# Decode attention on one core: TensorE's score matmuls rolled into an inner loop over pairs of groups, an empty first turn, and no loop aligned to a fetch block

## The chip, the cores and the metric

The kernel runs on one core of a Trainium2 chip. The metric is the device time of one execution in microseconds (us). Lower is better. The profile of the core lists five engines. The program has an instruction stream for each and orders them by semaphores: TensorE (PE; its weight loads are shown as PEld), VectorE (DVE), ScalarE (ACT), GpSimd (POOL) and SyncE (SP, which here issues the DMAs).

Every run in this study was in the fast state, with a granted TensorE clock of 1.000 wherever a profile gives it. The differences are small (under 0.3% in most runs), so most kernels were timed in five rounds beside runs of the kernel before on the same chip.

## The reference, cut to what matters

```python
B, Hq, Hkv, Sq, Sk, D = 1, 32, 8, 1, 65536, 128        # bf16
k = jnp.repeat(k, 4, axis=1); v = jnp.repeat(v, 4, axis=1)
scores = jnp.einsum("bhqd,bhkd->bhqk", q, k) * D ** -0.5
p = softmax(scores, axis=-1)
return jnp.einsum("bhqk,bhkd->bhqd", p, v)
```

There is one query per head, and 8 heads of K and V with 65536 rows each. K and V together are 268.4 MB and each byte is used once. The kernel cannot be faster than the stream of K and V from memory, 619.3 us at the 433.5 GB/s that the packets show (below).

## The kernel before

The work is cut into N = 16 chunks: 8 heads times 2 halves of 32768 rows. For each chunk, 8.39 MB of K and 8.39 MB of V are loaded. There are two K buffers and one V buffer. VectorE turns K by 16 transposes per chunk, one per "group" of 16 rows per partition, into two small buffers `ktb` used in turn. TensorE does 16 score matmuls per group into PSUM. ScalarE moves the scores out and takes the exponentials. TensorE then multiplies 256 weight tiles of V with them.

The DMA issues wait for the engines here:

```python
        def load_k(i):
            if i >= NK:
                sp.wait_ge(tr_s, (i - NK + 1) * G)      # K i-2 is transposed
            ...
        def load_v(i):
            if i < N - HALVED:
                if i >= 1:
                    sp.wait_ge(pv_s, 2 * i)             # values i-1 are done
                load(vbuf, vf, i, 0, T, v_in)
                return
            sp.wait_ge(pv_s, 2 * i - 1)                 # the last two V: in halves
            load(vbuf, vf, i, 0, TH, va_in)
            sp.wait_ge(pv_s, 2 * i)
            ...
```

TensorE before: one loop over chunks, aligned to a fetch block. The score matmuls of a chunk are written out, so their PSUM addresses are constants.

```python
        with nc.Fori(0, N + 1, 1, engines=..., head_slot={pe.engine: 0}) as it:
            ...                                          # registers of this turn
            hq = kept_ // C * QH
            qcols = [hq + be * A * R for be in range(NB * NE)]
            with pe.If_lt(turn, N):
                for g in range(G):                       # G = 16, unrolled
                    if g % GU == 0:
                        pe.wait_ge(mv_s, it * U + (g // GU + 1))
                    pe.wait_ge(tr_s, it * G + (g + 1))
                    scores(g, qcols)                     # 16 matmuls
            with pe.If_eq(skip, 0):                      # not in turn 0
                ...                                      # waits
                values(range(TH)) ...                    # 256 matmuls of chunk it-1
```

VectorE, for each group, waits until the score matmuls two groups back have read its buffer, and transposes:

```python
                    dv.wait_ge(qk_s, h * (C * G) + (b * G + g - NKT + 1))   # NKT = 2
                    transpose(b, g)
```

Of the kernel before, what the change touches and what calls it, by code (L numbers as in the profile page):

```python
# [5 lines left out]
DT = mybir.dt  # L6
AF = mybir.ActivationFunctionType
ALU = mybir.AluOpType
AX = mybir.AxisListType

P = 128
S4 = 32
T = 256
TG = 16
G = T // TG
U = 4
GU = G // U
NK = 2
NKT = 2
FIRST = (64, 64, 128)  # L20
KLAST = (128, 128)
VLAST = (72, 32, 16, 8)
NEND = 2
HALVED = 2


# [8 lines left out]
def bass_standalone__gqa_softmax__decode_kernel(nc, q, k, v, out):  # L35
    B, Hq, Sq, D = q.shape
    _, H, Sk, _ = k.shape
    R = Hq // H
    CK = P * T
    assert B == 1 and Sq == 1 and D == P and Hq == H * R == S4 and R == 4  # L40
    C = Sk // CK
    assert Sk % CK == 0 and C == 2
    N = H * C
    A = P // S4
    NB, NE = 2, 2
    W = T // U * R
    TH = T // 2
    QH = NB * NE * A * R
    scale = float(D) ** -0.5
    TE = sum(VLAST[-NEND:])  # L50
    assert sum(VLAST) == TH
# [5 lines left out]
    S = es.enter_context  # L57
# [6 lines left out]
    ktb = [sb(f"ktb{i}", [P, TG * D], DT.bfloat16) for i in range(NKT)]  # L64
# [23 lines left out]
    q4, qt = (scs[:, i * D // 2:(i + 1) * D // 2].bitcast(DT.bfloat16) for i in range(2))  # L88
    ident = ktb[0][:, 0:2 * P].bitcast(DT.float32)

    qkb = [S(nc.psum_tensor(f"qkb{i}", [P, 512], DT.float32)) for i in range(U)]
    acc = S(nc.psum_tensor("acc", [P, 512], DT.float32))

    def sem(name):
# [3 lines left out]
    v_in, va_in, vb_in = sem("v_in"), sem("va_in"), sem("vb_in")  # L98
    first_in = [sem(f"first_in{i}") for i in range(len(FIRST))]
    klast_in = [sem(f"klast_in{i}") for i in range(len(KLAST))]  # L100
    vlast_in = [sem(f"vlast_in{i}") for i in range(len(VLAST))]
# [12 lines left out]
    def pieces(sizes, at=0):  # L114
        for n, size in enumerate(sizes):
            yield n, at, at + size
            at += size
# [66 lines left out]

    @block.tensor
    def _(pe):
        def scores(g, qcols):


            kt = ktb[g % NKT][:, :].rearrange("p (b n e) -> p b e n", b=NB, e=NE)  # L190
            for n in range(TG // A):
                at = (g % GU * (TG // A) + n) * A * R
                for be in range(NB * NE):
                    ins = pe.matmul(  # L194
                        qkb[g // GU][:, at:at + A * R],
                        lhsT=kt[:, be // NE, be % NE, n * P:(n + 1) * P],
                        rhs=qblk[:, bass.ds(qcols[be], A * R)],
                        start=be == 0, stop=be == NB * NE - 1,
                    )
            ins.then_inc(qk_s, 1)  # L200

        def values(tiles):

            for t in tiles:
                ins = pe.matmul(  # L205
                    acc[:, 0:R], lhsT=vbuf[:, t * D:(t + 1) * D], rhs=pts[:, t * R:(t + 1) * R],
                    start=t == 0, stop=t == T - 1,
                )
                if t % TH == TH - 1:
                    ins.then_inc(pv_s, 1)  # L210


        turn, skip, skipl, late, last, kept, whole = (
            pe.alloc_register(name) for name in ("turn", "skip", "skipl", "late", "last", "kept", "whole"))
        pe.reg_mov(turn, 0)
        pe.wait_ge(qb_s, A * NB)
        with nc.Fori(
            0, N + 1, 1, engines=bass.OrderedEngineSet([pe.engine]), head_slot={pe.engine: 0},
        ) as it:
            pe.reg_alu(skip, it, 1, ALU.is_lt)  # L220
            pe.reg_alu(last, it, N, ALU.is_ge)
            pe.reg_alu(late, it, N - HALVED + 1, ALU.is_ge)
            pe.reg_add(skipl, skip, last)
            pe.reg_alu(kept, it, N - 1, ALU.min)
            pe.reg_alu(whole, it, N - HALVED, ALU.min)
            kept_ = pe.snap(kept, min_val=0, max_val=N - 1)
            whole_, late_, last_ = (pe.snap(r, min_val=0, max_val=N) for r in (whole, late, last))
            hq = kept_ // C * QH
            qcols = [hq + be * A * R for be in range(NB * NE)]
            with pe.If_lt(turn, N):  # L230
                for g in range(G):
                    if g % GU == 0:
                        pe.wait_ge(mv_s, it * U + (g // GU + 1))
                    pe.wait_ge(tr_s, it * G + (g + 1))
                    scores(g, qcols)
            with pe.If_eq(skip, 0):
                pe.wait_ge(co_s, it - 1)
                pe.wait_ge(ex_s, it * R)
                pe.wait_ge(v_in, whole_ * 16)
                pe.wait_ge(va_in, late_ * 16 + last_ * 16)  # L240
                values(range(TH))
                pe.wait_ge(vb_in, late_ * 16)
                for n, a, b in list(pieces(VLAST, TH))[:-NEND]:
                    pe.wait_ge(vlast_in[n], last_ * 16)
                    values(range(a, b))
            with pe.If_eq(skipl, 0):
                values(range(T - TE, T))
            pe.reg_add(turn, turn, 1)


        pe.wait_ge(tail_s, 2)
        pe.wait_ge(ow_s, H)
        pe.matmul(acc[:, 0:R], lhsT=ident, rhs=o2, start=False, stop=False)  # L253
        for n, a, b in list(pieces(VLAST, TH))[-NEND:]:
            pe.wait_ge(vlast_in[n], 16)
            values(range(a, b))

    @block.vector
    def _(dv):
# [47 lines left out]
            dv.alloc_register(name) for name in ("started", "before", "filled", "last"))  # L307


        with nc.Fori(0, H, 1, engines=bass.OrderedEngineSet([dv.engine]), head_slot={dv.engine: 0}) as h:  # L310
            dv.reg_alu(started, h, 1, ALU.is_ge)
            dv.reg_alu(last, h, H - 1, ALU.is_ge)
            dv.reg_alu(filled, h, 1, ALU.add)
            dv.reg_alu(filled, filled, H - 1, ALU.min)
            dv.reg_alu(before, h, -1, ALU.add)
            dv.reg_alu(before, before, 0, ALU.max)
            started_, last_ = dv.snap(started, min_val=0, max_val=1), dv.snap(last, min_val=0, max_val=1)
            filled_, before_ = dv.snap(filled, min_val=0, max_val=H - 1), dv.snap(before, min_val=0, max_val=H - 2)
            for b in range(C):
                dv.wait_ge(k_in[b], (filled_ if b else h) * 16)  # L320
                moved = h * (C * U) + (U + b * U + 1)
                for g in range(G):
                    for n, at, _ in pieces(KLAST if b else FIRST):
                        if at == g * TG:
                            dv.wait_ge((klast_in if b else first_in)[n], last_ * 16 if b else 16)
                    if b * G + g >= NKT:
                        dv.wait_ge(qk_s, h * (C * G) + (b * G + g - NKT + 1))  # L327
                    else:
                        dv.wait_ge(qk_s, h * (C * G) - started_ * (NKT - 1 - g))  # L329
                    transpose(b, g)  # L330
                    if g >= 2 * GU and g % GU == 0:
                        maximum(b, g // GU - 2, moved)
                for u in range(U - 2, U):
                    maximum(b, u, moved)
                dv.wait_ge(mx_s, h * (C * U) + (b + 1) * U)
                if b:
                    dv.wait_ge(hma_s, h * C + 1)
                dv.tensor_reduce(  # L338
                    hmax[:, b * R:(b + 1) * R], hp[b].rearrange("p (u g) -> p g u", g=R), AX.X, ALU.max,
                ).then_inc(hm_s, 1)  # L340
                if b:
                    dv.wait_ge(hma_s, h * C + 2)
                    dv.tensor_tensor(dif, mfirst, mtot, ALU.subtract).then_inc(df_s, 1)  # L343
                    dv.wait_ge(pv_s, h * (2 * C) + 2)
                    dv.tensor_copy(o1, acc[:, 0:R]).then_inc(co_s, 1)  # L345
                else:
                    with dv.If_eq(started, 1):
                        weigh(before_)
                        dv.wait_ge(pv_s, h * (2 * C))
                        dv.wait_ge(ow_s, h)  # L350
                        dv.tensor_tensor(o2, acc[:, 0:R], o2, ALU.add).then_inc(co_s, 1)  # L351
                        divisor(before_)
                        dv.wait_ge(co_s, h * C)
                        dv.tensor_tensor(oT[:, bass.ds(before_ * R, R)], o2, recip, ALU.mult).then_inc(fin_s, 1)  # L354
# [9 lines left out]
    def _(ac):  # L364
# [4 lines left out]
        ac.activation(warm[:, 8:9], warm[:, 9:10], AF.Exp, scale=1.0).then_inc(warm_s, 1)  # L369

        def move(b, u):
            fr = qkb[u][:, 0:W].rearrange("p (n a g) -> p a n g", a=A, g=R)
            to = scs[:, u * W:(u + 1) * W].rearrange("p (n x g) -> p x n g", x=A, g=R)
            for x in range(A):
                for a in range(A):
                    ins = ac.activation(to[a * S4:(a + 1) * S4, x, :, :], fr[x * S4:(x + 1) * S4, a, :, :], AF.Copy)  # L376
            ins.then_inc(mv_s, 1)


        with nc.Fori(0, H, 1, engines=bass.OrderedEngineSet([ac.engine]), head_slot={ac.engine: 0}) as h:  # L380
            for b in range(C):
                ac.wait_ge(ex_s, h * (C * R) + b * R)
                for u in range(U):
# [49 lines left out]
```

## Time and profile before

| | before |
|---|---|
| time, median | 629.28 us on the first three runs, 629.36 us with the three beside the kernel after |
| K and V moved | 268.45 MB; mean 428 GB/s over the span |
| busy: DVE / ACT / PE | 54% / 44% / 43% |
| mean rate in packets, 90 to 560 us | 433 GB/s |

From the page of the kernel before come the DMA rows in 40 slices and the costliest groups of instructions. In a group line the numbers after the bar are busy us and mean ns of one instruction; after the second bar comes the idle time before them and what ended most of it.

```profile
DMA  9999999999999999999999999999999999999997
GB/s 368 438 449 424 439 422 413 455 413 451 417 451 417 451 417 442 426 442 426 438 430 438 430 434 434 434 434 434 430 438 430 438 430 430 438 415 430 434 432 293
...
L276 DVE STREAM_TRANSPOSE ktb<-kbuf 128x1024 int32<-128x1024 int32 x256 | 295.7, 1212 | 155.8 <-DMA kbuf<-in_k_dram 142.3
...
L194 PE MATMUL qkb<-qblk,ktb 128*128 x4096 | 157.1, 176 | 341.4 <-DVE ktb L276 326.4
...
L205 PE MATMUL acc<-pts,vbuf 128*128 128x4 bf16 x4096 | 112.4, 166 | 14.1 <-DMA vbuf<-in_v_dram 13.4
```

The DMA engines are busy all the time and no other engine is. The large idle times are waits for data. The kernel is bound by the DMA stream: 268.45 MB at 433.5 GB/s take 619.3 us. The rest is the start, the end and any time at which the stream runs dry.

The chain of waits of the same kernel (start us, us, what) shows how one turn hangs together:

```profile
178.45 1.21 DVE ktb L276
179.71 0.59 PE qkb L194 x16
180.36 7.00 PE acc L205 x256
187.37 0.33 SPq L124
187.74 49.80 DMA kbuf<-in_k_dram
```

VectorE finishes the last transpose, TensorE the last scores and the values, then SP may issue the next V and K. The K so issued lands 49.8 us later, although 8.39 MB need only 19.4 us: the rest of the time it queues behind other transfers. The list of DMA issues (size or count, median us from issue to landing) says the same of V:

```profile
vbuf<-in_v_dram SPq DMA_DIRECT2D x14, 30.8
```

V needs 19.4 us of transfer, so it is issued while about 11 us of other load are still queued. As long as that queue does not run empty, time that TensorE loses costs nothing here.

There are two places where the queue is short. The first is early. Timeline of TensorE and SP (start us, us, engine, line, ..., count, [idle before, what ended it]):

```profile
52.48 1.32 PE L194 MATMUL qkb<-qblk,ktb 128*128 x32 [13.95 <-issue]
...
71.06 6.98 PE L205 MATMUL acc<-pts,vbuf 128*128 128x4 bf16 x256
...
78.08 0.33 SPq L124 DMA_DIRECT2D vbuf<-in_v_dram  x1
```

TensorE is idle for 14 us before its second chunk. One DMA queue, of the kind "instruction", carries nothing but five packets of 16 KB, about 1.0 us each; by their number and times they are TensorE's fetches. They start at 16.2, 31.6, 41.6, 48.6 and 55.9 us, the last three 7.0 and 7.3 us apart, with the DMA engines busy throughout (share 1.03 from 38 to 56 us); none comes later, though the loop runs 17 turns. The wait covers two of them. It makes the second V late (78.08 us), and the DMA engines then go partly idle.

The second place is the tail, where no K is left to load and the last V is loaded in halves, each waiting for values of the V before it. The timeline there:

```profile
596.36 0.59 PE L194 MATMUL qkb<-qblk,ktb 128*128 x16 [0.53 <-DVE ktb L276]
...
597.03 3.57 PE L205 MATMUL acc<-pts,vbuf 128*128 128x4 bf16 x128
600.63 10.22 SPq L124 DMA_DIRECT2D vbuf<-in_v_dram  x5
605.49 3.58 PE L205 MATMUL acc<-pts,vbuf 128*128 128x4 bf16 x128 [4.89 <-DMA vbuf<-in_v_dram]
```

The first half of the last V is issued at 600.63 us, when the first half of the values of chunk 14 is done. What was in flight then (the second half of V 14) lands at 605.49 us. The stream stays full, as the busy times of this stretch show (from, to, length; PE, PEld, DVE, ACT, POOL busy; clock; DMA share; GB/s):

```profile
600.00:610.00 10.00, 4.17 (x151) 4.00 (x148) 1.27 (x5) 1.89 (x8) 0.81 (x3) 1.00 1.01 433
```

### The profile page before, as it was taken

What the parts mean: (1) busy time and instruction counts of PE and PEld (TensorE: products, weight loads), DVE (VectorE), ACT (ScalarE), POOL (GpSimd) and SP (SyncE); (2) the same over time, 40 slices, a digit from 0 to 9 for tenths busy, and PEclk for the clock granted to TensorE, in tenths of its full rate; (3) what the DMA queues carried; (4) which work ended last, traced back from release to release, by engine and by line L of the source; (5) the groups of instructions that cost most, each with busy time, mean ns of one, the idle gap of its engine ahead of it and who ended that gap; (6) DMA issues with size and microseconds to landing.
All of it is one profiled execution on the core that took longest, in us unless ns stands there. A gap on an engine that the chain in (4) does not pass through costs nothing.

```text
span 628.1 us, 19282 instructions
## 1 busy us (share of the span) xinstructions
PE 269.9 (43%) x8194; PEld 243.9 (39%) x8194; DVE 341.2 (54%) x411; ACT 275.6 (44%) x1178; POOL 10.5 (2%) x32
## 2 busy tenths in 40 slices
PE   0323737144361534615346252452615526156445
PEld 0312636044361433614335152452514526146444
DVE  1865576290753908538094480935719357195910
ACT  0363645164351734517346172461725526264640
POOL 0000000000000000000000000000000000000000
DMA  9999999999999999999999999999999999999997
GB/s 368 438 449 424 439 422 413 455 413 451 417 451 417 451 417 442 426 442 426 438 430 438 430 434 434 434 434 434 430 438 430 438 430 430 438 415 430 434 432 293
DMA packets 6094, 268.60 MB, mean 428 GB/s; under 512 B 964, under 2 KB 964, under 8 KB 1220
## 3 DMA queue, kind: packets, MB, share of 16 engines
q1 hardware_dynamic: 5892, 268.45, 99.1%
q8 instruction: 5, 0.08, 0.1%
q10 hardware_dynamic: 192, 0.03, 0.0%
q14 instruction: 5, 0.04, 0.0%
HBM read 268.47 MB, written 0.01 MB: 427 GB/s over the span
## 4 chain that ended last, share of the span: by engine, by line
DMA 63%; DVE 16%; issue 10%; PE 10%; DVEq 0%; SPq 0%; ACTq 0%
DMA kbuf<-in_k_dram 55%; DVE ktb L276 14%; PE acc L205 9%; DMA vbuf<-in_v_dram 7%; DVE small L283 1%; DMA scs<-in_q_dram 1%; PE qkb L194 1%; SPq L124 0%; ACTq L366 0%; DVE qblk L271 0%; DVEq L329 0%; DVEq L327 0%; PE acc L253 0%; DVE scs L263 0%; DVE oTX L361 0%
## 5 line engine op out<-in xcount | busy, mean ns | idle before, releaser
L276 DVE STREAM_TRANSPOSE ktb<-kbuf 128x1024 int32<-128x1024 int32 x256 | 295.7, 1212 | 155.8 <-DMA kbuf<-in_k_dram 142.3
L376 ACT ACTIVATE scs<-qkb 32x64 f32<-32x64 f32 x1024 | 220.3, 215 | 280.2 <-PE qkb L194 269.0
L194 PE MATMUL qkb<-qblk,ktb 128*128 x4096 | 157.1, 176 | 341.4 <-DVE ktb L276 326.4
L194 PEld LDWEIGHTS qkb<-qblk,ktb 128*128 128x128 bf16 x4096 | 132.7, 105 | 365.7 <-issue 202.6
L205 PE MATMUL acc<-pts,vbuf 128*128 128x4 bf16 x4096 | 112.4, 166 | 14.1 <-DMA vbuf<-in_v_dram 13.4
L205 PEld LDWEIGHTS acc<-pts,vbuf 128*128 128x128 bf16 x4096 | 111.0, 104 | 15.7 <-DMA vbuf<-in_v_dram 11.6
L283 DVE TENSOR_REDUCE small<-scs 128x4 f32<-128x256 f32 x64 | 37.5, 586 | 61.4 <-ACT scs L376 61.4
L399 ACT ACTIVATE pts<-scs,small 128x256 bf16<-128x256 f32 x64 | 48.9, 853 | 30.7 <-PE acc L205 30.5
L171 POOL PARTITION_ALL_REDUCE small<-small x16 | 5.9, 370 | 589.9 <-DVE small L338 589.9
L399 ACT ACTIVATION_READ_ACCUMULATOR pts<-scs,small 128x1 f32 x64 | 13.6, 213 | 0.0
L387 ACT ACTIVATE small<-small 128x4 f32<-128x4 f32 x16 | 3.3, 206 | 22.5 <-POOL small L171 22.5
L345 DVE COPY small<-acc 128x4 f32<-128x4 f32 x8 | 1.3, 161 | 19.4 <-PE acc L205 19.4
L351 DVE TENSOR_TENSOR small<-acc,small 128x4 f32<-128x4 f32 x7 | 1.1, 163 | 13.8 <-PE acc L205 13.8
L359 DVE TENSOR_TENSOR oTX<-acc,small 128x4 bf16<-128x4 f32 x1 | 0.2, 163 | 12.3 <-PE acc L205 12.3
L263 DVE STREAM_TRANSPOSE scs<-scs 128x64 int32<-128x64 int32 x1 | 0.2, 246 | 9.8 <-DMA scs<-in_q_dram 9.8
L338 DVE TENSOR_REDUCE small<-small 128x4 f32<-128x16 f32 (+1 forms) x16 | 3.0, 185 | 1.3
L163 POOL PARTITION_ALL_REDUCE small<-small x8 | 3.4, 429 | 11.5 <-DVE small L296 11.5
L343 DVE TENSOR_TENSOR small<-small 128x4 f32<-128x4 f32 x8 | 1.3, 163 | 4.0 <-POOL small L171 4.0
L294 DVE TENSOR_TENSOR small<-small 128x4 f32<-128x4 f32 x8 | 1.3, 163 | 2.7 <-ACT pts L399 2.7
L369 ACT ACT_TABLE_LOAD x1 | 1.3, 1283 | 3.1 <-issue 3.1
L354 DVE TENSOR_TENSOR oTX<-small 128x4 f32 x7 | 1.1, 163 | 1.7 <-DVE small L300 1.7
L292 DVE TENSOR_TENSOR small<-small 128x4 f32<-128x4 f32 x8 | 1.4, 181 | 0.9
(18 smaller groups left out, 8.8 us busy)
## 6 DMA issues: line engine op xcount, KB each, us to landing
kbuf<-in_k_dram SPq DMA_DIRECT2D x3, 4096.0 KB, 40.2
vbuf<-in_v_dram SPq DMA_DIRECT2D x3, 4096.0 KB, 24.7
kbuf<-in_k_dram SPq DMA_DIRECT2D x2, 2048.0 KB, 10.3
vbuf<-in_v_dram SPq DMA_DIRECT2D x1, 2304.0 KB, 11.6
vbuf<-in_v_dram SPq DMA_DIRECT2D x1, 1024.0 KB, 13.7
vbuf<-in_v_dram SPq DMA_DIRECT2D x1, 512.0 KB, 14.5
vbuf<-in_v_dram SPq DMA_DIRECT2D x1, 256.0 KB, 14.6
kbuf<-in_k_dram SPq DMA_DIRECT2D x14, 49.8
```

Of the source, the lines that this page charges most:

```text
L163: g.partition_all_reduce(lsum, rhead, P, bass.bass_isa.ReduceOp.add).then_inc(ls_s, 1)
L171: g.partition_all_reduce(mtot if b else mfirst, hmax[:, b * R:(b + 1) * R], P, bass.bass_isa.ReduceOp.max,).then_inc(hma_s, 1)
L194: ins = pe.matmul(qkb[g // GU][:, at:at + A * R], lhsT=kt[:, be // NE, be % NE, n * P:(n + 1) * P], rhs=qblk[:, bass.ds(qcols[be], A * R)] ...
L205: ins = pe.matmul(acc[:, 0:R], lhsT=vbuf[:, t * D:(t + 1) * D], rhs=pts[:, t * R:(t + 1) * R], start=t == 0, stop=t == T - 1,)
L276: dv.transpose(to.rearrange("p (b t j) -> p b t j", b=NB, t=TG), fr.rearrange("p (t b i) -> p b t i", b=NB, t=TG),).then_inc(tr_s, 1)
L283: dv.tensor_reduce(hp[b][:, u * R:(u + 1) * R], scs[:, u * W:(u + 1) * W].rearrange("p (n g) -> p g n", g=R), AX.X, ALU.max,).then_inc(mx_ ...
L292: dv.tensor_tensor(o2, o1, wgt, ALU.mult).then_inc(ow_s, 1)
L294: dv.tensor_tensor(rhead, rsum[0], wgt, ALU.mult).then_inc(rw_s, 1)
L338: dv.tensor_reduce(hmax[:, b * R:(b + 1) * R], hp[b].rearrange("p (u g) -> p g u", g=R), AX.X, ALU.max,).then_inc(hm_s, 1)
L376: ins = ac.activation(to[a * S4:(a + 1) * S4, x, :, :], fr[x * S4:(x + 1) * S4, a, :, :], AF.Copy)
L387: ac.activation(negb[b], mtot if b else mfirst, AF.Copy, scale=-scale).then_inc(nb_s, 1)
L399: ac.activation(pv[:, g_, :], sv[:, g_, :], AF.Exp, bias=negb[b][:, g_:g_ + 1], scale=scale, accum_out=rsum[b][:, g_:g_ + 1],).then_inc(ex ...
```

## The change

The intent is to make TensorE's program small and to fetch it early. The 256 score matmuls of a chunk become 32 in a loop of 8 iterations. The value matmuls are cut into four conditional blocks, and a first turn that does nothing jumps through them, to fetch the code while TensorE would be waiting for data. The alignment of the loops on three engines goes. The core of the diff:

```diff
-    qkb = [S(nc.psum_tensor(f"qkb{i}", [P, 512], DT.float32)) for i in range(U)]
+    qkb = S(nc.psum_tensor("qkb", [P, U * BANK], DT.float32))
 ...
-                at = (g % GU * (TG // A) + n) * A * R
                 for be in range(NB * NE):
                     ins = pe.matmul(
-                        qkb[g // GU][:, at:at + A * R],
+                        qkb[:, bass.ds(at + n * A * R, A * R)],
 ...
-        pe.wait_ge(qb_s, A * NB)
-        with nc.Fori(
-            0, N + 1, 1, engines=bass.OrderedEngineSet([pe.engine]), head_slot={pe.engine: 0},
-        ) as it:
+        with nc.Fori(0, N + 2, 1, engines=engines) as it:
 ...
-            with pe.If_lt(turn, N):
-                for g in range(G):
-                    if g % GU == 0:
-                        pe.wait_ge(mv_s, it * U + (g // GU + 1))
-                    pe.wait_ge(tr_s, it * G + (g + 1))
-                    scores(g, qcols)
+            with pe.If_eq(skipk, 0):
+                pe.wait_ge(qb_s, A * NB)
+                hq = kb_ // C * QH
+                qcols = [hq + be * A * R for be in range(NB * NE)]
+                with nc.Fori(0, G // NKT, 1, engines=engines) as gp:
+                    upto = gp // (GU // NKT)
+                    at = gp * (NKT * TG * R) + upto * (BANK - W)
+                    pe.wait_ge(mv_s, kb_ * U + (upto + 1))
+                    for n in range(NKT):
+                        pe.wait_ge(tr_s, kb_ * G + (gp * NKT + (n + 1)))
+                        scores(ktb[n], at + n * TG * R, qcols)
 ...                                  (values in PVIF = 4 conditional blocks)
-        with nc.Fori(0, H, 1, engines=bass.OrderedEngineSet([dv.engine]), head_slot={dv.engine: 0}) as h:
+        with nc.Fori(0, H, 1, engines=bass.OrderedEngineSet([dv.engine])) as h:
 ...                                  (the same on ScalarE)
```

## The prediction

> **What bounds it now.** The DMA stream of K and V. The page gives 268.60 MB at 428 GB/s over a 628.1 us span; the DMA row is 9 in all but the last of 40 slices, and from 90 to 560 us packets move 433-434 GB/s. 268.45 MB / 433.5 GB/s = 619.3 us; the rest is the start (first K packet at 1.8 us, slow ramp), about 5 us after the last V piece (chain of waits) and small holes. PE (43% busy), DVE (54%) and ACT (44%) wait. In a steady turn, by the chain, K lands, 16 transposes take 19-20 us, values 7.00 us, then SP issues the next V. It lands after 30.8 us but needs 19.4 us of transfer (8.39 MB at 433 GB/s): some 11 us of load are still queued at issue[...]. That is PE's slack per chunk.

> **The one hole PE causes.** In its second turn PE idles 14.0 us (38.5 to 52.5 us, put down to issue). It has just jumped over turn one's value matmuls; the 16 KB instruction fetches lie at 16.2, 31.6, 41.6, 48.6 and 55.9 us, so this is two blocks through loaded rings, about 7 us each. Hence values 0 run at 71.1-78.0, V 1 is issued at 78.08, and the DMA runs partly dry at 80.2-81.3 us: 396 instead of 433 GB/s in that 10 us, a loss of 0.9 us. No later turn fetches: PE's five blocks stay resident. [...] DVE waits 6.0 us for its loop body at 12.5-18.5 us, which costs nothing, as transfers are queued to about 58 us.

> **What the change does.** Score code shrinks from 256 matmuls to 32, PE's stream from five fetched blocks to about three (estimate). The empty first turn touches them while PE would wait for the first transpose (20.0 us) anyway. DVE's loop head probably lies in a block already there, so transposes start some 5 us sooner. I expect the 14.0 us wait to go, V 1 to be issued by 73 us, and the hole to close: -0.9 us.

> Added: address arithmetic and a back edge per pair. [...] about 2.6 us, against DVE's 2.5 (two 1.13 us transposes, half a maximum). Scores then end 0.5-2 us later, inside the slack. Only the tail is tighter: the first half of the last V is issued at 600.6 us, the load ahead ends at 605.5, leaving about 2.6 us. If a pair takes p over 3.0 us, the DMA idles there by 4 x (p - 3.0) us: 20%.

> **Predicted time: 628.4 us**, 8 in 10 within 627.8 to 630.0. Faster by over 2%: 0.5%; within 2%: 97.5%; slower by over 2%: 2%.

> **Right or wrong, in the profile.** PE's issue wait near 38-52 us is gone and fetches lie before about 25 us; GB/s near 80 us is 433; K landings keep a 77.4 us period, about 1 us earlier; scores end at most 2 us later after a K landing; V's issue to landing stays near 31 us.

> **What would make it wrong.** [...] Register arithmetic several times my estimate. First scores later than 30 us. Tail code in a block that isn't resident (a few us).

A pair came to about 2.6 us: 2 x 0.59 us of matmuls, which the trace of the kernel before shows, and the estimate for the register operations and the back edge. The room of about 2.6 us in the tail had allowances in it: 600.6 to 605.5 us is 4.9 us, so 2.3 us were taken off. (The traces show 1.03 us from the issue of the first K to its first packet, 0.74 to 1.77 us in the kernel before, and 0.96 us for the first half of the last V, 604.06 to 605.02 us in the kernel after.) The predicted time: 629.28 - 0.9 = 628.4 us.

## The result

| | median us | runs |
|---|---|---|
| before | 629.36 | 629.05 to 629.64, 6 runs |
| after | 630.43 | 630.39 to 630.61, 6 runs |

The ratio is 1.0018, with a 95% interval of 1.0005 to 1.0030: slower by about 1.1 us and outside the range of the prediction. (Ratios here are the mean time of one kernel's fast runs over that of the other's of the same rounds, so they are not quite the ratios of the medians.)

The page of the kernel after, the same rows and groups:

```profile
DMA  9999999999999999999999999999999999999987
GB/s 367 438 459 413 454 413 454 413 454 413 454 413 454 413 454 413 454 421 446 421 446 421 446 421 446 421 446 421 446 421 446 421 446 421 446 410 433 431 365 303
...
L293 DVE STREAM_TRANSPOSE ktb<-kbuf 128x1024 int32<-128x1024 int32 x256 | 303.1, 1222 | 137.6 <-DMA kbuf<-in_k_dram 112.0
...
L195 PE MATMUL qkb<-qblk,ktb 128*128 x4096 | 216.1, 180 | 278.1 <-DVE ktb L293 241.2
```

The same matmuls of the scores keep TensorE busy for 216.1 us instead of 157.1. The stream has a new dip in the last but one slice (365 GB/s).

The early place, in the timeline of the kernel after:

```profile
45.17 1.70 PE L195 MATMUL qkb<-qblk,ktb 128*128 x32 [9.28 <-DVE ktb L293]
...
66.54 6.98 PE L206 MATMUL acc<-pts,vbuf 128*128 128x4 bf16 x256 [0.55 <-issue]
...
73.55 0.33 SPq L126 DMA_DIRECT2D vbuf<-in_v_dram  x1
```

The second chunk's scores start at 45.2 instead of 52.5 us and wait for a transpose, not for code. The second V is issued at 73.55 us, and the sum of the packets has no loss left in 70-90 us. TensorE's fetches are now two, at 6.7 and 13.6 us. This part went as predicted.

The cadence of the scores did not. The timeline of the kernel before in the middle of a chunk, groups one by one:

```profile
557.86 0.59 PE L194 MATMUL qkb<-qblk,ktb 128*128 x16 [0.53 <-DVE ktb L276]
558.22 4.61 DVE L276 STREAM_TRANSPOSE ktb<-kbuf 128x1024 int32<-128x1024 int32 x4
559.51 0.59 PE L194 MATMUL qkb<-qblk,ktb 128*128 x16 [1.06 <-DVE ktb L276]
560.64 0.59 PE L194 MATMUL qkb<-qblk,ktb 128*128 x16 [0.53 <-DVE ktb L276]
```

The timeline of the kernel after, at the start of the last chunk's scores, two groups (32 matmuls) in a line:

```profile
579.06 1.69 PE L195 MATMUL qkb<-qblk,ktb 128*128 x32 [2.38 <-DVE ktb L293]
580.15 2.37 DVE L293 STREAM_TRANSPOSE ktb<-kbuf 128x1024 int32<-128x1024 int32 x2 [0.28 <-PE qkb L195]
581.72 1.69 PE L195 MATMUL qkb<-qblk,ktb 128*128 x32 [0.96 <-DVE ktb L293]
582.80 2.37 DVE L293 STREAM_TRANSPOSE ktb<-kbuf 128x1024 int32<-128x1024 int32 x2 [0.28 <-PE qkb L195]
```

Before, a group's 16 matmuls take 0.59 us and VectorE transposes without a pause, one group per 1.13 us. After, a pair takes 2.66 us (579.06 to 581.72), and VectorE is idle 0.28 us before each pair of transposes, waiting for TensorE ("PE qkb L195"). The first 16 matmuls of a pair take 1.05 us (the lines split by group show 1.03 to 1.05), the second 0.65. V's issue to landing shows what that adds up to over a chunk:

```profile
vbuf<-in_v_dram SPq DMA_DIRECT2D x14, 27.9
```

It was 30.8 us. TensorE is 2.9 us later in every chunk, and in the steady turns the queue absorbs it: the packets keep 433 GB/s from 90 to 560 us. In the tail it does not:

```profile
598.20 1.68 PE L195 MATMUL qkb<-qblk,ktb 128*128 x32 [0.81 <-ACT scs L393]
...
600.46 3.57 PE L206 MATMUL acc<-pts,vbuf 128*128 128x4 bf16 x128 [0.59 <-issue]
604.06 6.20 SPq L126 DMA_DIRECT2D vbuf<-in_v_dram  x5
604.84 3.57 PE L206 MATMUL acc<-pts,vbuf 128*128 128x4 bf16 x128 [0.81 <-DMA vbuf<-in_v_dram]
```

The busy times of the same stretch as before, for the kernel after:

```profile
600.00:610.00 10.00, 7.14 (x256) 6.98 (x256) 1.28 (x5) 5.31 (x23) 0.81 (x3) 1.00 0.80 318
```

(Some lines name ScalarE as the one that ended TensorE's wait. The semaphore that they mean asks for moves of the chunk before, done long ago; a move of this chunk only happened to end at that moment. The wait that held TensorE is for the transpose.)

The first half of the last V is issued at 604.06 us, 3.43 us later than before, while the load ahead of it lands at 604.7 us. That is only its last part: its 16 completion signals came between 602.98 and 604.72 us, eleven of them by 603.31, so most of the stream had run dry before the next load was issued. The DMA share of 600-610 us falls from 1.01 to 0.80. Summing the packets, the 16 engines are idle for 2.16 us on average between 598 and 612 us (before: none). The last packet of V comes 1.10 us later than before (625.70 against 624.59 us), and from there to the end both kernels take the same time.

So the theory after reading was: the pair loop delays each chunk by 2.9 us; the tail alone cannot hide it and loses 2.2 us; the early hole gives back about 0.6 us (0.33 us in 70-90 us and 0.25 us in 20-70 us, where fetches took the place of data: four of about 1.0 us each over 16 engines are 0.26 us). The rivals were that the missing alignment or the empty turn costs time, that the loop costs time all along the run, and, inside the theory, that the delay comes from the branch and not from the address arithmetic.

### The profile page after: what moved, and what is told of

It reads as the page before. It is cut to its first block, busy times and chain, and to the rows that moved or that the text cites. A ratio compares the mean times of both kernels' runs of the same rounds, so it can differ in the third digit from the quotient of the medians.

```text
span 629.1 us, 21215 instructions
## 1 busy us (share of the span) xinstructions
PE 329.0 (52%) x8194; PEld 294.3 (47%) x8194; DVE 348.4 (55%) x411; ACT 275.6 (44%) x1178; POOL 10.5 (2%) x32
## 3 DMA queue, kind: packets, MB, share of 16 engines
q1 hardware_dynamic: 5892, 268.45, 98.9%
## 4 chain that ended last, share of the span: by engine, by line
DMA 61%; PE 18%; ACT 11%; DVE 5%; issue 4%; SPq 0%; DVEq 0%; ACTq 0%
DMA kbuf<-in_k_dram 52%; ACT scs L393 11%; PE qkb L195 10%; PE acc L206 9%; DMA vbuf<-in_v_dram 7%; DVE ktb L293 5%; DMA scs<-in_q_dram 2%; SPq L126 0%; ACTq L383 0%; DVEq L346 0%; DVE qblk L288 0%; PE acc L270 0%; DVE small L300 0%; DVE scs L280 0%; DVE oTX L378 0%
## 5 line engine op out<-in xcount | busy, mean ns | idle before, releaser
L293 DVE STREAM_TRANSPOSE ktb<-kbuf 128x1024 int32<-128x1024 int32 x256 | 303.1, 1222 | 137.6 <-DMA kbuf<-in_k_dram 112.0
L195 PE MATMUL qkb<-qblk,ktb 128*128 x4096 | 216.1, 180 | 278.1 <-DVE ktb L293 241.2
L195 PEld LDWEIGHTS qkb<-qblk,ktb 128*128 128x128 bf16 x4096 | 183.0, 107 | 311.0 <-issue 292.0
L416 ACT ACTIVATION_READ_ACCUMULATOR pts<-scs,small 128x1 f32 x64 | 13.6, 212 | 0.0
## 6 DMA issues: line engine op xcount, KB each, us to landing
vbuf<-in_v_dram SPq DMA_DIRECT2D x1, 2304.0 KB, 13.3
vbuf<-in_v_dram SPq DMA_DIRECT2D x1, 512.0 KB, 16.2
```

What stands on the lines that cost most here:

```text
L195: ins = pe.matmul(qkb[:, bass.ds(at + n * A * R, A * R)], lhsT=kt[:, be // NE, be % NE, n * P:(n + 1) * P], rhs=qblk[:, bass.ds(qcols[be], ...
L293: dv.transpose(to.rearrange("p (b t j) -> p b t j", b=NB, t=TG), fr.rearrange("p (t b i) -> p b t i", b=NB, t=TG),).then_inc(tr_s, 1)
L416: ac.activation(pv[:, g_, :], sv[:, g_, :], AF.Exp, bias=negb[b][:, g_:g_ + 1], scale=scale, accum_out=rsum[b][:, g_:g_ + 1],).then_inc(ex ...
```

## The experiments

All kernels gave correct results. "Hole" below is the mean idle time of the 16 DMA engines from the sum of packet times. It is computed from the trace of one profiled execution each.

### e1: scores unrolled again

The kernel after, with only the pair loop undone:

```diff
-                with nc.Fori(0, G // NKT, 1, engines=engines) as gp: ...
+                for g in range(G):
+                    if g % GU == 0:
+                        pe.wait_ge(mv_s, kb_ * U + (g // GU + 1))
+                    pe.wait_ge(tr_s, kb_ * G + (g + 1))
+                    scores(ktb[g % NKT], g // GU * BANK + g % GU * (TG * R), qcols)
-                        qkb[:, bass.ds(at + n * A * R, A * R)],
+                        qkb[:, at + n * A * R:at + (n + 1) * A * R],
```

> The kernel after with the pair loop unrolled again (fixed addresses), the empty first turn kept and no loop aligned. Tail theory (the pair loop makes scores end about 2.7 us later per chunk, so in the tail the first half of the last V is asked for too late and the DMA idles 2.2 us at 602-605 us; the empty turn gains about 0.6 us early): no tail hole, early hole still closed, 628.3 us (628.0 to 628.7). Rival (the loss comes from the empty turn or the missing alignment): 630.2 us or more, as after.

Measured: 628.87 us (before, same rounds: 629.24; ratio 0.9992, 0.9979 to 1.0006). The values of chunk 14 start at 596.54 us, there is no tail hole, and the early hole stays closed. The time lies 0.2 us above the stated range's edge. The pair loop accounts for the loss, about 1.6 us from e1 to after; the rest of the change is a small gain.

### e4 and e4b: a tail that waits for no values

In e4 the pair loop stays, but the last V goes into the K buffer that chunk 14 has left, so that its issue waits for transposes that are long done. The values of chunk 15 then follow the loop and read that buffer. In e4b the same is done to the kernel before.

```diff
+            if i == N - 1:
+                sp.wait_ge(tr_s, (N - 1) * G)
+                load(kbuf[i % NK - 1], vf, i, 0, TH, vk_in)
+                ...                                     # and its last pieces
+                return
             sp.wait_ge(pv_s, 2 * i - 1)
```

Both first versions were refused by the check: a wait on a shared semaphore could be met by either of two loads. They were mended with a semaphore of its own.

> The kernel after with its slow pair loop, but the last chunk of V is loaded into the K buffer that chunk 14 has left, so its issue no longer waits for any value matmul. Tail theory: pairs still take 2.66 us, V 15 is issued right behind V 14, the DMA has no hole after 20 us, time 628.2 us (627.8 to 628.6). Rival (the pair loop or the fetching costs time all along the run): still about 630.4 us.

> Control: the same tail on the kernel before, which had no tail hole. Tail theory: same as before, 629.1-629.4 us, with the early hole at 80 us (0.3-0.9 us) still there. If the new tail is a gain of its own, it is over 0.5 us faster than before, and the run of the same tail on the kernel after proves less.

Measured: e4 628.73 us (ratio 0.9991, 0.9977 to 1.0005). The timeline of e4 shows TensorE as late as in the kernel after, and the last V issued 27 us sooner:

```profile
577.09 2.33 SPq L126 DMA_DIRECT2D kbuf<-in_v_dram  x5
...
600.51 3.57 PE L208 MATMUL acc<-pts,vbuf 128*128 128x4 bf16 x128 [0.59 <-issue]
```

The busy times of e4 in the tail have a full stream again:

```profile
600.00:610.00 10.00, 7.14 (x256) 6.98 (x256) 1.28 (x5) 5.43 (x23) 0.81 (x3) 1.00 0.99 426
```

The time is 0.1 us above the stated range. The slow loop costs nothing where the tail does not wait for it. That settles the place of the loss. The rival of a cost all along the run falls.

e4b missed its expectation: 630.27 us, with an unusual spread (629.46 to 631.01), against 629.24. The new tail shows no gain of its own, so e4 is not explained by it. Why it is slower on the kernel before stays open; its early hole is nearly gone (0.05 us in 70-90 us), so that is not the reason. Its profile has two more instruction fetches at 620.9 and 625.2 us, near the end of the stream, and the DMA engines finish less evenly (about 1.5 us idle after 612 us against 0.7). But e4 has such fetches too (618.9 and 622.4 us) without the loss.

### e3: the address arithmetic ahead of the wait

After, plus 8 throw-away matmuls before the wait for the transposes, which use the same address registers, so that the wait is followed by matmuls alone:

```diff
                     pe.wait_ge(mv_s, kb_ * U + (upto + 1))
+                    for n in range(NKT * TG // A):
+                        pe.matmul(qkb[:, bass.ds(at + n * A * R, A * R)], lhsT=qblk[:, 0:P],
+                                  rhs=qblk[:, bass.ds(qcols[n % (NB * NE)], A * R)], start=True, stop=True)
```

> The kernel after, with 8 throw-away matmuls ahead of the wait for the transposes of each pair, which use the same address registers, so that all address arithmetic is done before the wait and not between wait and matmuls. If that arithmetic is what makes the first 16 matmuls of a pair take 1.05 instead of 0.59 us: they fall to 0.6-0.7, the pair from 2.66 to about 2.3 us, VectorE's 0.3 us waits on the matmuls go, the tail hole falls under 0.6 us and the time to 628.4-628.9. If the loop's own branch and waits are the cost: 1.05 and 2.66 stay or grow, 630.4 or more.

Measured: 629.66 us (ratio 1.0005, 0.9991 to 1.0018).

The timeline of e3, with the throw-away matmuls (x8) and the real ones (x32) of one pair:

```profile
135.37 1.21 PE L244 MATMUL qkb<-qblk 128*128 x8 [0.36 <-issue]
136.57 1.02 PE L195 MATMUL qkb<-qblk,ktb 128*128 x32
```

The 32 real matmuls of a pair now take 1.02 us instead of 1.69, so the arithmetic is what stretched them. But the 8 throw-away matmuls with their arithmetic take 1.2 us of TensorE themselves, so the pair keeps about 2.6 us and the expectation of 2.3 us was wrong. The tail hole shrinks to 1.28 us, not to under 0.6, and the time lies 0.8 us above the range.

### e9: more register arithmetic

After, plus 32 register operations and one wait that is always met (33 operations, six instructions once the compiler has fused them), between the wait of a pair and its first matmuls:

```diff
                         pe.wait_ge(tr_s, kb_ * G + (gp * NKT + (n + 1)))
+                        if n == 0:
+                            for _ in range(16):
+                                pe.reg_alu(turn, turn, 1, ALU.add)
+                                pe.reg_alu(turn, turn, A * NB, ALU.min)
+                            pe.wait_ge(qb_s, turn)
```

> The kernel after with six more fused register instructions (33 more register operations) between the wait and the first matmuls of each pair. If such an instruction costs about 58 ns there (0.46 us for the 8 that the loop has): first 16 matmuls start 0.35 us later, pair 2.66 to about 3.0 us, 2.8 us more per chunk, of which both of the last two chunks feel it: tail hole 2.2 to about 7 us (5 to 9), 634-637 us. If register work is hidden behind the matmul queue: pair stays 2.66, 630.4 us.

(The 0.46 us in it are the 1.05 us of a pair's first 16 matmuls less the 0.59 us of the kernel before.)

Measured: 656.58 us (ratio 1.0424, 1.0408 to 1.0440).

The timeline of e9, two pairs with the transposes between them:

```profile
86.27 1.68 PE L195 MATMUL qkb<-qblk,ktb 128*128 x32 [3.48 <-DVE ktb L298]
87.34 2.37 DVE L298 STREAM_TRANSPOSE ktb<-kbuf 128x1024 int32<-128x1024 int32 x2 [1.09 <-PE qkb L195]
89.73 1.71 PE L195 MATMUL qkb<-qblk,ktb 128*128 x32 [1.78 <-DVE ktb L298]
```

The pair goes from 2.66 to 3.46 us and VectorE's wait from 0.28 to 1.09 us: 0.80 us for 33 operations, 24 ns each on average. The direction was as expected, the size was not: 0.35 us had been expected. From a chunk's first transpose to its last score it is now 28.3 us, 5.9 us more than in the kernel after. By the packets the DMA runs dry in six of some twelve steady turns, for 0.2 to 1.8 us each (5 us in sum); 3.5 us are lost early and 14 us in the tail.

The start times of the single matmuls in the kernel after (medians over chunks 3 to 12) show where the time goes. Four of the six instructions in the first group follow one matmul each, and there the next matmul starts 0.12 to 0.13 us after the one before, instead of 0.03 to 0.05: 0.37 us in sum. The other two, and all three of the second group, follow four matmuls and cost about 0.02 us each. In e3 the real matmuls stand 0.03 to 0.05 us apart throughout. So it is the four closely spaced address computations at the head of an iteration that cost.

### e2 and e11: four groups per iteration

```diff
-                with nc.Fori(0, G // NKT, 1, engines=engines) as gp: ...
+                with nc.Fori(0, U, 1, engines=engines) as u:
+                    at = u * BANK
+                    pe.wait_ge(mv_s, kb_ * U + (u + 1))
+                    for n in range(GU):
+                        pe.wait_ge(tr_s, kb_ * G + (u * GU + (n + 1)))
+                        scores(ktb[n % NKT], at + n * TG * R, qcols)
```

e11 is e2 with the outer loop started at 1, without the empty turn.

> The kernel after with the inner loop over four groups (4 iterations per chunk in place of 8). The extra time per chunk comes once per iteration, so it is halved: scores end about 1.4 us later than unrolled instead of 2.7; tail hole 0 to 0.6 us; time 628.6-629.3 us.

> The quad loop without the empty turn. Run e6 says that the empty turn is worth nothing: 628.6-628.9 us as with it, no early hole, no tail hole.

Measured: e2 628.74 us (before, same rounds: 629.33; ratio 0.9991, 0.9978 to 1.0004), e11 628.76 us (before 629.43; 0.9988, 0.9974 to 1.0001). Values of chunk 14 start at 597.31 us in e2, and neither has a tail hole. A loop as such is harmless here: with four iterations per chunk it takes 628.74 us, with eight (after) 630.43 us. In e2 the first group of an iteration shows the same four gaps of 0.12 to 0.13 us (16 matmuls starting over 0.85 us), and the other three groups hardly any (0.48 us; 0.42 in the kernel before).

### e7 and e8: a delay without a loop

e1 with 36 or 112 throw-away matmuls into a spare bank between scores and values of each chunk:

```diff
+            with pe.If_eq(skipk, 0):
+                for _ in range(36):                      # e8: 112
+                    pe.matmul(idle[:, 0:R], lhsT=qblk[:, 0:P], rhs=qblk[:, 0:R], start=True, stop=True)
```

> e1 (unrolled scores, empty first turn) with 36 throw-away matmuls into a spare bank between scores and values of every chunk: about 36 x 27.3 ns = 1.0 us more TensorE work per chunk. Tail theory: inside the slack of about 2.4 us, no hole, 628.7-629.1 us as e1. If any TensorE time added per chunk shows in the total (16 us in sum), it is clearly slower.

> The same with 112 throw-away matmuls, about 3.1 us per chunk, the size of the pair loop's delay, but without any loop. Tail theory: no hole before 600 us, a hole of about 2 us (1 to 3) at 602-606 us, time 630.0-631.5 us. If it is the loop itself (fetches, branches) that costs time and not the delay, 628.9 as e1.

(The 27.3 ns of e7's expectation are 7.00 us over the 256 value matmuls of a chunk.)

Measured: e7 628.76 us (before 629.33; ratio 0.9990, 0.9977 to 1.0003): 17.6 us more of matmuls in sum, and no change. e8 633.43 us (ratio 1.0081, 1.0066 to 1.0096; two of its six runs were near 636 us). The tail hole is there, but it is 1.08 us and not 2; the larger part of the loss is an early hole of 3.14 us, which I had not expected. The longer code has five blocks to fetch, TensorE starts its first scores only at 28.95 us (transposes had begun at 13.47 us), and the second V is late. A plain delay of the size of the pair loop's does open the tail hole, but e8 mixes it with an early one, so it gives the kind of effect and not its size.

### e6, e5 and e10: the empty turn and the alignment

```diff
 e6, on after:   -with nc.Fori(0, N + 2, 1, engines=engines) as it:
                 +with nc.Fori(1, N + 2, 1, engines=engines) as it:
 e5, on after:   + head_slot={...: 0} on the three outer loops again
 e10, on before: - head_slot={...: 0} on its three loops
```

> The kernel after, starting its outer loop at 1: no empty first turn. If the empty turn is what closes the early hole: TensorE stalls for a fetch of 5-8 us after the first scores at about 36 us, but scores start at 15 us either way; with chunk 1's K landing at 43.6 us the stall is largely hidden, so 630.3-630.8 us, at most 0.4 us slower than after. The tail hole of 2.2 us stays.

> The kernel after with all three outer loops aligned to a fetch block again. If the missing alignment costs anything in the long run: faster than after. Tail theory: VectorE's first transpose comes later (17-19 us, as before, instead of 13.3), nothing else of weight changes, tail hole still 2.2 us, 630.2-630.7 us, like after.

> The kernel before with its three loops no longer aligned, nothing else. If leaving out the alignment is what closes the early hole (first transposes at 12-13 instead of 18.5 us, so the two fetches after the first scores fall into the wait for K 1): scores of chunk 1 start at 45-48 instead of 52.5 us, second V issued at 71-74 us, no early hole, no tail hole, 628.7-629.1 us. If the empty turn or the smaller code is needed: early hole as before, 629.2-629.4 us.

Measured: e6 630.29 us (before 629.33; ratio 1.0015, 1.0002 to 1.0028), e5 630.88 us (before 629.43; 1.0021, 1.0007 to 1.0034), e10 628.79 us (before 629.43; 0.9987, 0.9974 to 1.0001). Each of e6 and e5 has the tail hole (2.22 and 2.41 us), and none of the three the early one. e5 ended 0.2 us above its range. The timeline of e10, with the first transposes, the first values and the second V:

```profile
12.15 9.28 DVE L276 STREAM_TRANSPOSE ktb<-kbuf 128x1024 int32<-128x1024 int32 x8
...
63.66 6.99 PE L205 MATMUL acc<-pts,vbuf 128*128 128x4 bf16 x256
70.68 0.33 SPq L124 DMA_DIRECT2D vbuf<-in_v_dram  x1
```

Leaving out the alignment is enough to close the early hole on the old code: transposes start at 12.15 instead of 18.54 us, the first scores end 5 us sooner, and the fetches that follow them fall into the wait for K. On the new code the empty turn adds nothing to that (e6). On the old, long code it even holds the first scores back: TensorE starts them at 22.7 us in e1, and at 13.6 us in e10. With aligned loops, as in e5, the early hole is closed too, though the first transpose comes as late as before (18.71 us); whether by the empty turn or by the smaller code, no run tells apart. So there is more than one way to close it. Leaving out the alignment is enough by itself (e10), and no run shows a gain beyond that.

### All tails together

| run | first half of values 14 starts, us | tail hole, us |
|---|---|---|
| e1 | 596.54 | 0 |
| before | 597.03 | 0 |
| e2 | 597.31 | 0 |
| e3 | 599.54 | 1.28 |
| after | 600.46 | 2.16 |
| e6 | 600.46 | 2.22 |
| e5 | 600.94 | 2.41 |

From e3 to after the start moves by 0.92 us and the hole by 0.88. Carried back along that line (an estimate for the kernel after, from two points), the hole opens at about 598.2 us, only 1.2 us after the start in the kernel before.

The hole is 2.16 us but after is only about 1.6 us slower than e1 and e10. In the runs without a tail hole the engines finish less evenly: they are idle 1.0 to 1.2 us on average after 612 us in e1, e2, e4, e7, e10 and e11 (0.7 in the kernel before), against 0.1 to 0.3 in the runs with one of over 2 us. Why was not tested.

e1, e2, e4, e10 and e11 beat both kernels by their medians, by 0.4 to 0.7 us against before. The intervals of their ratios just include 1, though each of their runs was faster than every run of the kernel before in the same rounds.

## Why the prediction was wrong

- **Bound by the stream, with slack in the steady turns: right.** 2.9 us of delay per chunk changed nothing between 90 and 560 us (433 GB/s in both), and e7 and e4 show the same. e9, about 8.8 us later per chunk than the kernel before (28.3 against 20.0 us to the last score, 0.5 us into the values), is at its edge: the DMA ran dry in half of its turns.
- **The early hole closes: right, with a smaller gain and partly another cause.** I put it at 0.9 us; the packets show about 0.6 (0.33 in 70-90 us and 0.25 in 20-70). e10 is 0.6 us faster than before by the medians too, but that is not the same sum: it still makes four fetches in 20-70 us, so only the 0.33 is accounted for there. I gave the credit to the empty turn; e6 and e10 show that leaving out the alignment is enough. In e10 the earlier first transpose, which the prediction named only in passing, is what moved; e5 shows that the empty turn and the smaller code close the hole without it.
- **"About 2.6 us, against DVE's 2.5": the pair time was right (2.66 us), its use was wrong.** I compared two rates as if the slower engine alone set the pace. With two buffers and the arithmetic after the wait, the times add: 1.26 us for the first transpose of a pair, 0.31 us to the first matmul, 1.05 us for the first 16 matmuls, then 0.04 us until VectorE goes on: 2.66 us in sum. VectorE's maxima (0.57 us per four groups) come on top, so four groups take 5.56 us where they took 5.03.
- **"Scores then end 0.5-2 us later": the first mis-sized term.** They ended 2.4 us later (20.0 to 22.4 us from a chunk's first transpose to its last score), and the way into the values took 0.5 us more: 2.9 us from a K landing to the next V issue.
- **The tail, "leaving about 2.6 us" and "4 x (p - 3.0)": the second mis-sized term, and the step that failed.** By that formula a pair of 2.66 us leaves no hole; there was one of 2.16 us. Above all the delay was too small: I had counted only the last four pairs of chunk 15, because K's last piece lands late in the kernel before. But chunk 14 is late too, and VectorE starts chunk 15 only after the values that follow chunk 14's scores. The delay at the first half of values 14 was 1.07 us from the later start of chunk 15's transposes (576.42 to 577.49), 1.84 us from slower pairs (first transpose to last score: 20.54 to 22.38 us), and 0.52 us from the longer way into the values (0.07 to 0.59 us): 3.43 us. The room was too large as well: the hole opens after about 1.2 us (the estimate above). The load ahead ends 0.7 us sooner (604.7 against 605.4), 0.5 us of it because the early hole is gone (604.9 in e10), and I had counted to its last part, when most of it was done at 603.3.
- **Late first scores, tail code that is not resident: neither came true in the kernel after.** Its first scores start at 15.00 us, and it has two 16 KB fetches, at 6.7 and 13.6 us, and none later. In the kernel before, TensorE stood 14.0 us at a jump to code not yet fetched, with two blocks to fetch.
- **The sign.** I expected -0.9 us and gave the tail 20%. The sum was about -0.5 us (e1 or e10) and +1.6 us.

## What to carry to other kernels

This stream hid an engine's delay only while loads were queued behind it: 2.9 us per chunk cost nothing with about 11 us of load queued (433 GB/s in both kernels), and the tail lost 2.16 us. So look at the tail separately, where the last loads wait for the last work and the delays of the last two chunks add up (3.43 us here). With two buffers between two engines, add what lies between a wait and its release on both sides before comparing rates (2.66 us a pair here, where VectorE alone needs about 2.5). Address computations ahead of the wait left the matmuls behind it at 1.02 us for the 32 of a pair (e3; 1.69 us in the kernel after), though the throw-away matmuls that carried them took 1.2 us; several matmuls apart they cost about 0.02 us each, close together about 0.1 us; and a longer loop body has fewer heads of iterations (e2, no tail hole). When a change has three parts, run each alone: here the smallest one, leaving out an alignment, gave all of the gain by itself (e10, 0.6 us by the medians).
